# New prices in a list scheduler, and a third engine for the centring of rows: banded attention and a SoLU layer on one core

## The chip, the core and the metric

The kernel runs on one core of one Trainium2 chip. The core has a matrix engine (PE, with its weight loads listed apart as PEld), a vector engine (VectorE, DVE), an activation engine (ScalarE, ACT), GpSimd (POOL) and a sync engine (SP) that here issues loads. All run their own instruction streams in order and wait for each other by semaphores. The metric is the device time of one execution in microseconds (us), the median of several runs.

## The reference

Four batches of 8 heads with 768 positions and 64 columns each. A row of queries sees a band of 31 keys and, beside them, one summary key for each of 24 blocks of 32 positions (the maximum of the block's keys, with the mean of its values). The attention's output, 3072 rows of 512, goes through a layer with a softmax-weighted activation, a layer norm and a second product.

```python
k_sum = k.reshape(B, H, nb, 32, D).max(axis=3)
v_sum = v.reshape(B, H, nb, 32, D).mean(axis=3)
scores_l = where(abs(i - j) < 16, scale * q @ k.T, -1e9)
scores_s = scale * q @ k_sum.T + log(32)
a = softmax(concat([scores_l, scores_s]))
x = (a @ concat([v, v_sum])) as (3072, 512)
h = x @ w_in                                  # (3072, 1024)
solu = h * softmax(h)
mu = mean(solu); var = mean((solu - mu) ** 2)
out = ((solu - mu) / sqrt(var + 1e-6) * g_ln) @ w_out
```

## The kernel before

The 3072 rows are 24 tiles of 128. The kernel does not issue instructions as it meets them. Each step is recorded by `op(engine, cost, fn, ...)` as an operation with a planned cost in us, the buffers that it reads and writes, and at times other engines that could do it (`alt`, each with its own cost and function). At the end `Plan.issue` (L131) walks a planned clock: it takes the operation that can start first, on ties the one whose result is due first, gives it an engine and calls its function. So the costs decide two things, the order of the instructions in each engine's stream and which engine gets an operation that has a choice. They change no instruction's own duration on the chip.

An engine is passed over for an operation when another of its engines would have it done earlier, start plus cost plus a surcharge `DEAR` (L82, L154 to L166). An operation with `port=True` is one that VectorE, by the planner's assumption, can't run while GpSimd runs. Its planned cost on VectorE has the rest of GpSimd's current operation added, up to `HELD` (L150). A planned transfer ends by `RATE`. Until a planned time of `FILL` = 80 us, idle time of the matrix engine is filled with products of zeros (`keep_up`, L209; they appear in the profile as line L802).

The stages that matter:

- The loads, on SP's queue: keys and queries of batch 0, eight pieces of `w_in`, rows of values, then `w_out`.
- The weights come as 64-bit numbers, 16 pieces of 128x512. `rounded` (L313) makes 32-bit numbers of each: two scalings (L322, L328, on ScalarE or VectorE), a shift (L333) and a bit-wise combination (L337) on VectorE, and an integer add on GpSimd (L341, the only engine it has). Each `w_in` piece is then split in a high part (a copy with three helper lines, L245 to L247, one for each engine) and a low part (a subtraction by `tt`, L252 on VectorE or L253 on GpSimd). `w_out` is split by L363 and L365.
- Attention, for half a group of 256 positions at a time: `kw` gathers the windows of keys (`COPY_K`) and the maxima (`COPY_KS`), PE makes scores `s` (L505), VectorE masks them and takes maxima (L525), ScalarE takes exponentials (L533), and `e` is scaled by its sums (`MUL_E`, by `tt`: L252 on VectorE, L253 on GpSimd). Then PE turns it (`t`, L561) and makes `x` (L599).
- For a tile, `first(t)` (L613): `h` on PE (L625, 24 products), maximum (L632, VectorE), exponentials (L634, ScalarE), the product with its sum (L638, VectorE), minus the mean (`nmu`, L641), and then the centring: `he` plus `nmu` in two halves of 512 columns, each on GpSimd (L645) or VectorE (L647). ScalarE's squares (L650) follow. GpSimd takes a power (L655).
- `turn(t)` (lt, L561; lh, ll by L675) and `second(t)` (o, L690, 24 products) come three tiles later; the result leaves by L695 or L697 and a transfer from ScalarE's queue (L699).
- `add_rows` (L425) sums rows of values of the next batch on GpSimd, in halving steps.

The prices of the operations with a choice, before:

```python
COPY_W = ((act, 0.52), (dve, 0.34))
COPY_K = ((act, 0.74), (dve, 0.47))
COPY_KS = ((pool, 0.6), (dve, 0.19))
COPY_P = ((act, 0.48), (dve, 0.6))
LO_W = ((dve, 0.6), (pool, 1.4))
MUL_E = ((pool, 1.8), (dve, 1.07))
```

Of the kernel before, what the change touches and what calls it, by code (L numbers as in the profile page):

```python
# [31 lines left out]
WIN = QT + 2 * HALO  # L32
# [37 lines left out]
class Plan:  # L70
# [5 lines left out]

    RATE = 360.0
    START = 0.7
    COLD, FILL = 6.9, 80.0
    IDLE = 0.22  # L80
    WAIT, FAR = 1.5, 200
    DEAR = {"dve": 0.7, "act": 0.3}  # L82
    HELD = 1.1
    SYNC = 0.13
# [46 lines left out]
    def issue(self):  # L131
        ready, free, then, dma = {}, {}, {}, 0.0
        for o in self.ops:
# [87 lines left out]
def attn_then_solu(ctx: ExitStack, tc: tile.TileContext, q, k, v, vb, w_in, w_out, g_ln, out):  # L221
# [91 lines left out]
    def rounded(key, st, part):  # L313
# [32 lines left out]
    def split_w_in(c, nh):  # L346
        if nh == 0:
# [25 lines left out]
    def load_keys(b, p, after=()):  # L373
        pp, i = divmod(p, 2)
        if i == 0:
            kraw[b, pp] = plan.buf(sb, [P, 2, SP], F32, "kraw", 3, f"kraw{b}_{pp}")
        x = kraw[b, pp]
        op(sp, 0.05, lambda: nc.sync.dma_start(out=x.ap[:, i], in_=k[b, p]), w=[(x, i)], nbytes=P * SP * 4,
           after=after)
# [11 lines left out]
    def load_v_rows(b, i):  # L391

        rows = v[b, HALO + 2 * P * i:HALO + 2 * P * (i + 1), :].rearrange("(c p) n -> p c n", p=P)
        vst[b, i] = x = plan.buf(sb, [P, 2, 512], F32, "lh" if i < 2 else "ll", 2, f"st_v{b}_{i}")
        op(sp, 0.05, lambda: nc.sync.dma_start(out=x.ap, in_=rows), w=[x], nbytes=P * 4096)

# [16 lines left out]
    def add_rows(b, hh, i):  # L413

        x = plan.buf(sb, [P, 1024], F32, "vrow", 2, f"st_v{b}_{hh}_{i}")
        n, w = NB * 4, BLOCK * D // 2
        op(sp, 0.05, lambda w=w: nc.sync.dma_start(out=x.ap[:n, :w], in_=vb[b, hh, :, i * w:(i + 1) * w]),
           w=[x], nbytes=P * 4096)
# [29 lines left out]
    def load_q(b, g, pairs=None, after=()):  # L448
# [4 lines left out]
        if pairs is None:  # L453
            op(sp, 0.05, lambda: nc.sync.dma_start(out=x.ap, in_=src), w=[x], nbytes=P * 4096,
               after=after)
        else:
            op(sp, 0.05, lambda: nc.sync.dma_start(out=x.ap[:, pairs], in_=src[:, pairs]),
               w=[(x, pairs)], nbytes=P * 1024)

    def load_v(b, g, after=()):  # L460
        vt[b, g] = x = plan.buf(sb, [P, G, DM], F32, "vt", 2, f"vt{b}_{g}")
        rows = v[b, g * G * QT:g * G * QT + WIN, :]
        src = bass.AP(rows.tensor, rows.offset, [[DM, WIN], [QT * DM, G], [1, DM]])
        op(sp, 0.05, lambda: nc.sync.dma_start(out=x.ap[:WIN], in_=src), w=[(x, 0)], nbytes=WIN * 8192,
           after=after)
# [147 lines left out]
    def first(t):  # L613
# [29 lines left out]
        for hf in range(2):  # L643
# [3 lines left out]
               r=[nmu], w=[(e, hf)], alt=[(dve, 0.4, lambda sl=sl: nc.vector.tensor_scalar(  # L647
                out=e.ap[:, sl], in0=e.ap[:, sl], scalar1=nmu.ap, scalar2=None, op0=ALU.add))])
        sq = plan.buf(sb, [P, DF], BF16, "sq", 1, f"sq{t}")
# [30 lines left out]
    def second(t):  # L680
# [3 lines left out]
        for cols in [slice(0, 256), slice(256, 512)] if t == NT - 1 else [slice(0, DM)]:  # L684
            k = (cols.stop - cols.start) / DM
            o = plan.buf(ps, [P, DM], F32, "x", 2, f"o{t}")
            for f in range(NFC):
                def mm(f=f, w=wo[f], o=o, cols=cols):
# [24 lines left out]
    for x in LOADS:  # L713
        first_loads[x].pop(0)()
    op(sp, 0.05, lambda: nc.sync.dma_start(out=g_sb, in_=g_ln), w=[g_b], nbytes=P * 64)
    for pp in range(NPP):
# [121 lines left out]
```

## Time and profile before

| what | value |
|---|---|
| median of 3 runs | 412.13 us (410.32 to 412.26) |
| the profiled execution | 411.95 us, of which its span in the trace is 410.2 us |
| granted PE clock, mean | 0.988 |
| instructions | 9471 |
| PE, PEld busy | 392.3 us (96%), 302.7 us (74%) |
| DVE, ACT, POOL busy | 285.7 us (70%), 234.8 us (57%), 119.7 us (29%) |
| HBM read, written | 36.97 MB, 6.29 MB |

Busy time of PE has the products of zeros of L802 in it. The trace names a group of instructions by its line, engine and operation, then what it writes and reads. The time of an instruction that waits inside its engine, for a port say, counts as its duration. Idle time is told apart by what ended it (`<-`).

### The profile page before, as it was taken

Reading aid. Unit: us, or ns where it says so; the run is one execution under the profiler, and the core shown is the slowest. Engines: PE = TensorE matmul, PEld = TensorE weight load, DVE = VectorE, ACT = ScalarE, POOL = GpSimd, SP = SyncE. Lnnn points to the kernel's source line nnn. Section 1 sums busy time; section 2 is a strip of 40 time slices with the busy share of each in tenths; the row PEclk is TensorE's granted clock in tenths of the full one; section 3 lists DMA queues with packets and bytes.
Section 4 is the critical chain, followed back from the end, with each engine's and each line's share of the span. In section 5 each row is a group of like instructions: output and inputs, shape, how many; then the busy total and the mean of one; then the engine's idle time right before and its main releaser. Section 6 shows DMA issues by size and latency. Waiting matters only on the chain.

```text
span 410.2 us, 9471 instructions
## 1 busy us (share of the span) xinstructions
PE 392.3 (96%) x3666; PEld 302.7 (74%) x3666; DVE 285.7 (70%) x849; ACT 234.8 (57%) x704; POOL 119.7 (29%) x170
## 2 busy tenths in 40 slices
PE   6999798798999999999999999999999999999996
PEld 2436576576777777887788888887888888887776
DVE  4999898997667796657876766665684876455520
ACT  4967987765567666464654654746755464123321
POOL 4576545877573001011611111101101100111000
PEclk9998999998999999999999999999999999999999
DMA  8999995226444805017416023044030000000011
GB/s 264 410 269 270 329 267 159 93 78 193 121 137 126 212 27 153 2 41 202 120 51 166 2 81 99 24 103 98 27 95 29 26 2 27 27 26 25 2 51 53
DMA packets 22929, 46.03 MB, mean 112 GB/s; under 512 B 1860, under 2 KB 8260, under 8 KB 22884
## 3 DMA queue, kind: packets, MB, share of 16 engines
q1 hardware_dynamic: 18096, 36.97, 31.8%
q10 hardware_dynamic: 4788, 8.46, 6.5%
q8 instruction: 29, 0.48, 0.5%
q14 instruction: 16, 0.13, 0.1%
HBM read 36.97 MB, written 6.29 MB: 105 GB/s over the span
## 4 chain that ended last, share of the span: by engine, by line
PE 69%; DVE 8%; DMA 2%; ACT 2%; issue 0%; ACTq 0%; DVEq 0%
PE o L690 31%; PE h L625 25%; PE x L599 4%; PE s L505 4%; PE lt L561 3%; DMA kraw<-in_k 2%; PE t L561 2%; DVE ksum L387 2%; DVE hm L632 1%; PE vs_ps L440 1%; DVE cv_out L333 1%; DVE ll L675 1%; ACT e L533 1%; DVE e L525 1%; DVE w L365 1%; DVE he L638 1%
## 5 line engine op out<-in xcount | busy, mean ns | idle before, releaser
L625 PE MATMUL h<-w,xh 128*128 128x512 f32 x384 | 126.9, 400 | 5.3 <-DVE he L638 5.2
L690 PE MATMUL o<-w,lh 128*128 128x512 f32 (+1 forms) x400 | 128.3, 393 | 0.0
L533 ACT ACTIVATE e<-e,nm 128x120 f32<-128x120 f32 x192 | 73.1, 384 | 30.7 <-DVE nm L525 30.7
L625 PEld LDWEIGHTS h<-w,xh 128*128 128x128 f32 x384 | 72.7, 189 | 24.2 <-DVE he L638 4.1
L690 PEld LDWEIGHTS o<-w,lh 128*128 128x128 f32 x400 | 74.0, 188 | 18.8 <-issue 2.4
L690 PE MATMUL o<-w,ll 128*128 128x512 f32 (+1 forms) x200 | 77.4, 387 | 0.0
L625 PE MATMUL h<-w,xl 128*128 128x512 f32 x192 | 76.0, 396 | 0.0
L645 POOL TENSOR_SCALAR he<-he,nmu 128x512 f32<-128x512 f32 x23 | 20.9, 909 | 119.0 <-DVE nmu L641 109.4
L245 ACT COPY at<-t 120x512 f32<-120x512 f32 x47 | 25.2, 587 | 47.4 <-PE t L561 46.3
L632 DVE TENSOR_REDUCE hm<-h 128x1 f32<-128x1024 f32 x24 | 29.3, 1221 | 25.9 <-PE h L625 25.9
L690 PEld LDWEIGHTS o<-w,ll 128*128 128x128 f32 x200 | 37.6, 188 | 7.4
L650 ACT ACTIVATE sq<-he 128x1024 bf16<-128x1024 f32 x24 | 25.4, 1058 | 29.8 <-POOL he L645 16.7
L625 PEld LDWEIGHTS h<-w,xl 128*128 128x128 f32 x192 | 36.4, 189 | 7.9
L525 DVE CUSTOM_DVE_ANT_0 e<-s,mask 128x120 f32<-128x120 f32 x192 | 40.6, 275 | 2.3 <-PE s L505 2.3
L675 DVE TENSOR_TENSOR ll<-lt,lh 128x512 fp32r<-128x512 f32 x48 | 31.9, 684 | 8.1 <-ACT lh L245 7.6
L533 ACT ACTIVATION_READ_ACCUMULATOR e<-e,nm 128x1 f32 x192 | 36.4, 190 | 0.0
L425 POOL TENSOR_TENSOR st_v<-st_v 96x512 f32<-96x512 f32 (+3 forms) x42 | 32.1, 778 | 12.6 <-DMA st_v<-in_vb 12.0
L634 ACT ACTIVATE he<-h,hm 128x1024 f32<-128x1024 f32 x24 | 27.0, 1126 | 10.8 <-DVE hm L632 10.7
L638 DVE SCALAR_TENSOR_TENSOR he<-h,hz,he 128x1024 f32<-128x1024 f32 x24 | 30.6, 1277 | 0.2
L599 PE MATMUL x<-at,vt 120*64 120x64 f32 (+1 forms) x768 | 29.5, 230 | 0.7 <-ACT at L245 0.6
L599 PEld LDWEIGHTS x<-at,vt 120*64 120x64 f32 (+1 forms) x768 | 25.5, 141 | 6.1 <-issue 2.6
L247 POOL COPY kw<-ksum 128x192 f32<-128x192 f32 (+1 forms) x26 | 8.7, 337 | 71.9 <-ACT lh L245 31.7
(80 smaller groups left out, 513.2 us busy)
## 6 DMA issues: line engine op xcount, KB each, us to landing
vt<-in_v SPq DMA_DIRECT2D x12, 768.0 KB, 5.9
kraw<-in_k SPq DMA_DIRECT2D x16, 400.0 KB, 4.6
out<-os ACTq DMA_DIRECT2D x23, 256.0 KB, 2.0
qt<-in_q SPq DMA_DIRECT2D x11, 512.0 KB, 7.2
st_v<-in_vb SPq DMA_DIRECT2D x12, 384.0 KB, 4.9
raw<-in_w_in SPq DMA_DIRECT2D x8, 512.0 KB, 7.5
raw<-in_w_out SPq DMA_DIRECT2D x8, 512.0 KB, 12.7
vt<-vsum ACTq DMA_DIRECT2D x11, 192.0 KB
```

What stands on the lines that cost most here:

```text
L245: by = {act: lambda: nc.scalar.copy(out=to(), in_=of()), dve: lambda: nc.vector.tensor_copy(out=to(), in_=of()), pool: lambda: nc.gpsimd.t ...
L425: op(pool, 0.15 + w * 0.0021, lambda w=w, o=o: nc.gpsimd.tensor_tensor(out=o.ap[:n, :w], in0=x.ap[:n, :w], in1=x.ap[:n, w:2 * w], op=ALU.add),
L525: nc.vector.tensor_tensor_reduce(out=e.ap[:, n, :], in0=sc.ap[:, j, (2 * i + up) * KC:(2 * i + up + 1) * KC], in1=mask[:, mi, :], scale=-S ...
L533: nc.scalar.activation(out=e.ap[:, n, :], in_=e.ap[:, n, :], func=AF.Exp, bias=nm.ap[:, n:n + 1], scale=-1.0, accum_out=z.ap[:, n:n + 1])
L599: nc.tensor.matmul(xp.ap[j * D:(j + 1) * D, i, qs], vs.ap[:k, u, cs], at.ap[:k, u % 2, n[j] + u // 2, :], start=not apart, stop=not apart ...
L625: nc.tensor.matmul(o, a.ap[:, c, ts], w.ap[:, i], start=(c == 0 and n == 0), stop=(c == NKC - 1 and n == 2))
L632: op(dve, 1.13, lambda: nc.vector.tensor_reduce(out=nm.ap, in_=h.ap, op=ALU.max, axis=AX.X, negate=True), r=[h], w=[nm])
L634: op(act, 1.09, lambda: nc.scalar.activation(out=e.ap, in_=h.ap, func=AF.Exp, bias=nm.ap, accum_out=z.ap), r=[h, nm], w=[e, z])
L638: op(dve, 1.27, lambda: nc.vector.scalar_tensor_tensor(out=e.ap, in0=h.ap, scalar=z.ap, in1=e.ap, op0=ALU.mult, op1=ALU.mult, accum_out=s1 ...
L650: op(act, 1.13, lambda: nc.scalar.activation(out=sq.ap, in_=e.ap, func=AF.Square, accum_out=ss.ap), r=[e], w=[sq, ss])
L675: op(dve, 0.6, lambda part=part, r=r: nc.vector.tensor_tensor(out=part(lo), in0=tp.ap[:, r], in1=part(hi).bitcast(F32), op=ALU.subtract), ...
L690: nc.tensor.matmul(o.ap[:, cols], a.ap[:, f, :], w.ap[:, i, cols], start=(f == 0 and n == 0), stop=(f == NFC - 1 and n == 2))
```

## The change

It has three parts.

1. The transfers. The planned rate goes from one value to two (270 up to a planned 6.9 us, 400 after it), a transfer's tail from 0.8 to 0.6, and the cost of issuing one from 0.05 to 0.43 us on SP's queue and from 0.06 to 0.34 or 0.8 on ScalarE's.
2. The port. VectorE's port operations are charged the whole rest of GpSimd's operation, and GpSimd's operations the rest of VectorE's last port operation (`held`). More of VectorE's operations count as port operations: L337, the low parts of both weights, the centring. `DEAR` goes from 0.7 to 0.6 for VectorE, stays 0.3 for ScalarE and is 1.0 for GpSimd, which had none.
3. The centring has a third choice, an `activation` with a bias on ScalarE, at 0.57.

```diff
-    RATE = 360.0
+    RATE, SLOW = 400.0, 270.0
-    DEAR = {"dve": 0.7, "act": 0.3}
-    HELD = 1.1
+    DEAR = {"dve": 0.6, "act": 0.3, "pool": 1.0}
...
         def cost(e, o, t):
-            held = min(max(free.get("pool", 0.0) - t, 0.0), self.HELD) if e == "dve" and o.port else 0.0
-            return o.can[e][0] * (2 if e == "pe" and t < self.COLD else 1) + held
+            other = free.get("pool", 0.0) if e == "dve" and o.port else held if e == "pool" else 0.0
+            return o.can[e][0] * (2 if e == "pe" and t < self.COLD else 1) + max(other - t, 0.0)
...
             o.end = free[e] = t + cost(e, o, t)
+            if e == "dve" and o.port:
+                held = o.end
             if o.nbytes:
-                dma = max(dma, o.end + 1.0) + o.nbytes / self.RATE * 1e-3
-                o.end = dma + 0.8
+                dma = max(dma, o.end + 1.0)
+                dma += o.nbytes / (self.RATE if dma > self.COLD else self.SLOW) * 1e-3
+                o.end = dma + 0.6
...
-        op(sp, 0.05, lambda: nc.sync.dma_start(out=x.ap, in_=src.bitcast(I32)), w=[x], nbytes=P * 4096,
+        op(sp, 0.43, lambda: nc.sync.dma_start(out=x.ap, in_=src.bitcast(I32)), w=[x], nbytes=P * 4096,
...
         op(dve, 0.6, lambda: nc.vector.scalar_tensor_tensor(
             out=low(), in0=high(), scalar=-2 ** 31, in1=low(), op0=ALU.bitwise_and, op1=ALU.bitwise_or),
-            r=[(x, 1)], w=[(x, 0)])
+            r=[(x, 1)], w=[(x, 0)], port=True)
...
         tt(LO_W, ALU.subtract, lambda: hl.ap[:, 1], w, lambda: hl.ap[:, 0].bitcast(F32),
-           r=[(st, nh), (hl, 0)], w=[(hl, 1)])
+           r=[(st, nh), (hl, 0)], w=[(hl, 1)], port=True)
...
-            op0=ALU.mult, op1=ALU.subtract), r=[(st, f % 2), (hl, 0), g_b], w=[(hl, 1)])
+            op0=ALU.mult, op1=ALU.subtract), r=[(st, f % 2), (hl, 0), g_b], w=[(hl, 1)], port=True)
...
-        return op(act, 0.06, lambda: nc.scalar.dma_start(
+        return op(act, 0.8, lambda: nc.scalar.dma_start(
...
                r=[nmu], w=[(e, hf)], alt=[(dve, 0.4, lambda sl=sl: nc.vector.tensor_scalar(
-                out=e.ap[:, sl], in0=e.ap[:, sl], scalar1=nmu.ap, scalar2=None, op0=ALU.add))])
+                out=e.ap[:, sl], in0=e.ap[:, sl], scalar1=nmu.ap, scalar2=None, op0=ALU.add)),
+                (act, 0.57, lambda sl=sl: nc.scalar.activation(
+                    out=e.ap[:, sl], in_=e.ap[:, sl], func=AF.Identity, bias=nmu.ap))], port=True)
...
-            op(act, 0.06, lambda os=os, cols=cols: nc.scalar.dma_start(
+            op(act, 0.34, lambda os=os, cols=cols: nc.scalar.dma_start(
```

The other loads on SP's queue change from 0.05 to 0.43 in the same way.

More of the change, by code (lines that the diff above doesn't have):

```diff
@@ L131, in issue @@
     def issue(self):
-        ready, free, then, dma = {}, {}, {}, 0.0
+        ready, free, then, dma, held = {}, {}, {}, 0.0, 0.0
         for o in self.ops:
@@ L377, in load_keys @@
         x = kraw[b, pp]
-        op(sp, 0.05, lambda: nc.sync.dma_start(out=x.ap[:, i], in_=k[b, p]), w=[(x, i)], nbytes=P * SP * 4,
+        op(sp, 0.43, lambda: nc.sync.dma_start(out=x.ap[:, i], in_=k[b, p]), w=[(x, i)], nbytes=P * SP * 4,
            after=after)
@@ L394, in load_v_rows @@
         vst[b, i] = x = plan.buf(sb, [P, 2, 512], F32, "lh" if i < 2 else "ll", 2, f"st_v{b}_{i}")
-        op(sp, 0.05, lambda: nc.sync.dma_start(out=x.ap, in_=rows), w=[x], nbytes=P * 4096)
+        op(sp, 0.43, lambda: nc.sync.dma_start(out=x.ap, in_=rows), w=[x], nbytes=P * 4096)
     def mean_values_first(b):
@@ L416, in add_rows @@
         n, w = NB * 4, BLOCK * D // 2
-        op(sp, 0.05, lambda w=w: nc.sync.dma_start(out=x.ap[:n, :w], in_=vb[b, hh, :, i * w:(i + 1) * w]),
+        op(sp, 0.43, lambda w=w: nc.sync.dma_start(out=x.ap[:n, :w], in_=vb[b, hh, :, i * w:(i + 1) * w]),
            w=[x], nbytes=P * 4096)
@@ L453, in load_q @@
         if pairs is None:
-            op(sp, 0.05, lambda: nc.sync.dma_start(out=x.ap, in_=src), w=[x], nbytes=P * 4096,
+            op(sp, 0.43, lambda: nc.sync.dma_start(out=x.ap, in_=src), w=[x], nbytes=P * 4096,
                after=after)
         else:
-            op(sp, 0.05, lambda: nc.sync.dma_start(out=x.ap[:, pairs], in_=src[:, pairs]),
+            op(sp, 0.43, lambda: nc.sync.dma_start(out=x.ap[:, pairs], in_=src[:, pairs]),
                w=[(x, pairs)], nbytes=P * 1024)
@@ L463, in load_v @@
         src = bass.AP(rows.tensor, rows.offset, [[DM, WIN], [QT * DM, G], [1, DM]])
-        op(sp, 0.05, lambda: nc.sync.dma_start(out=x.ap[:WIN], in_=src), w=[(x, 0)], nbytes=WIN * 8192,
+        op(sp, 0.43, lambda: nc.sync.dma_start(out=x.ap[:WIN], in_=src), w=[(x, 0)], nbytes=WIN * 8192,
            after=after)
@@ L714, in attn_then_solu @@
         first_loads[x].pop(0)()
-    op(sp, 0.05, lambda: nc.sync.dma_start(out=g_sb, in_=g_ln), w=[g_b], nbytes=P * 64)
+    op(sp, 0.43, lambda: nc.sync.dma_start(out=g_sb, in_=g_ln), w=[g_b], nbytes=P * 64)
     for pp in range(NPP):
```

## The prediction

> **What bounds the kernel now.** I read the page's first part for the shares, then the windows, to see whether one limit holds all along.
>
> ```profile
> span 410.2 us, 9471 instructions
> ...
> 10.00:94.00 84.00, 73.85 (x691) 48.33 (x684) 80.21 (x195) 65.49 (x186) 53.67 (x53) 0.96 0.79 232
> ...
> 94.00:100.00 6.00, 6.00 (x87) 4.82 (x86) 4.00 (x21) 2.58 (x5) 3.33 (x6) 0.72 0.64 169
> 100.00:400.00 300.00, 298.83 (x2789) 240.29 (x2788) 197.65 (x625) 161.14 (x506) 57.76 (x91) 1.00 0.27 74
> 400.00:410.20 10.20, 7.08 (x55) 6.55 (x53) 0.00 (x0) 1.64 (x3) 0.00 (x0) 1.00 0.15 53
> ```
>
> After the width the columns are busy PE, PEld, DVE, ACT, POOL, then granted clock, share of the DMA engines and GB/s. There are two regimes. From 100 to 400 PE is idle for 1.17 of 300 us, so no order of the other engines can save more than that there. From 10 to 94 VectorE is busy for 80.21 of 84 us, and PE's 73.85 has products of zeros in it. The chain of waits and PE's waits say the same:
>
> ```profile
> 71.73 2.89 DVE cv_out L333
> ...
> 92.26 1.30 DVE he L638 x2
> 93.56 0.14 issue
> 93.70 1.24 PE h L625 x3
> ```
>
> ```profile
> PE h L625 <- DVE he L638: 5.2, 3, 1.9
> ```
>
> Up to 93.70 the chain that ends last runs on VectorE, then on PE, and the first tiles' `h` wait for the product L638 that frees the one `h` buffer. Since PE's work behind that point is fixed, the end moves about as far as VectorE's stage ends earlier or later. The change has to be judged there.
>
> VectorE's time in this stage is not all work. VectorE's rows, then GpSimd's (start, duration; in brackets the idle time before it and what ended it):
>
> ```profile
> 12.71 0.68 DVE L337 SCALAR_TENSOR_TENSOR raw<-raw 128x512 int32<-128x512 int32 x1
> 15.41 2.28 DVE L337 SCALAR_TENSOR_TENSOR raw<-raw 128x512 int32<-128x512 int32 x1
> 20.88 2.00 DVE L252 TENSOR_TENSOR e<-e,z 128x960 f32<-128x960 f32 x1
> 23.40 0.42 DVE L333 TENSOR_SCALAR cv_in<-raw 128x512 int32<-128x512 int32 x1
> 25.77 1.78 DVE L337 SCALAR_TENSOR_TENSOR raw<-raw 128x512 int32<-128x512 int32 x1
> 27.47 1.51 DVE L333 TENSOR_SCALAR cv_in<-raw 128x512 int32<-128x512 int32 x1
> 28.91 1.78 DVE L337 SCALAR_TENSOR_TENSOR raw<-raw 128x512 int32<-128x512 int32 x1
> 35.77 0.68 DVE L252 TENSOR_TENSOR w<-cv_in,w 128x512 fp32r<-128x512 f32 x1
> 40.90 1.25 DVE L333 TENSOR_SCALAR cv_out<-raw 128x512 int32<-128x512 int32 x1
> 71.65 2.97 DVE L333 TENSOR_SCALAR cv_out<-raw 128x512 int32<-128x512 int32 x1
> 86.26 1.21 DVE L647 TENSOR_SCALAR he<-he,nmu 128x512 f32<-128x512 f32 x1
> ```
>
> ```profile
> 15.29 1.86 POOL L253 TENSOR_TENSOR e<-e,z 128x960 f32<-128x960 f32 x1 [0.17 <-DVE z L539]
> 20.54 1.32 POOL L253 TENSOR_TENSOR w<-cv_in,w 128x512 fp32r<-128x512 f32 x1 [1.37 <-ACT raw L322]
> 25.59 1.41 POOL L341 TENSOR_TENSOR cv_in<-cv_in,raw 128x512 int32<-128x512 int32 x1 [0.63 <-DVE raw L337]
> 26.96 3.18 POOL L253 TENSOR_TENSOR w<-cv_in,w 128x512 fp32r<-128x512 f32 x2
> 40.57 1.30 POOL L253 TENSOR_TENSOR w<-cv_in,w 128x512 fp32r<-128x512 f32 x1 [1.76 <-ACT w L245]
> 71.22 1.78 POOL L253 TENSOR_TENSOR e<-e,z 128x960 f32<-128x960 f32 x1
> 72.98 1.35 POOL L645 TENSOR_SCALAR he<-he,nmu 128x512 f32<-128x512 f32 x2
> 85.39 1.79 POOL L253 TENSOR_TENSOR e<-e,z 128x960 f32<-128x960 f32 x1
> ```
>
> L337 takes 0.68 with GpSimd idle and 1.78 when it starts 0.18 behind an add of 1.41: it sits out GpSimd's instruction. At 71.65 a shift of 0.42 lasts 2.97, through one product and two centrings on GpSimd.
>
> **The change part by part.** *Which work changes engine.* The rule adds the surcharge to the cost. Low parts: GpSimd 1.4 + 1.0 against VectorE 0.6 + 0.6 (before 1.4 against 1.3). Scaling of `e`: 1.8 + 1.0 against 1.07 + 0.6 (before 1.8 against 1.77). Maxima into `kw`: 1.6 against 0.79 (before 0.6 against 0.89). Centring: GpSimd 1.62, VectorE 1.0, ScalarE 0.87 (before 0.62 and 1.1). GpSimd now needs VectorE busy with non-port work for 1.2, 1.1 or 0.8 us to win one of these. I take it that all of them leave GpSimd in this stage and that a tile's first half is centred on ScalarE and its second on VectorE. What stood there:
>
> ```profile
> L253 POOL TENSOR_TENSOR e<-e,z 128x960 f32<-128x960 f32 x4 | 7.2, 1804 | 1.6 <-DVE z L539 1.6
> L253 POOL TENSOR_TENSOR w<-cv_in,w 128x512 fp32r<-128x512 f32 x4 | 5.8, 1460 | 3.1 <-ACT w L245 1.8 <-ACT raw L322 1.4
> ...
> L645 POOL TENSOR_SCALAR he<-he,nmu 128x512 f32<-128x512 f32 x3 | 2.0, 689 | 0.0
> L247 POOL COPY kw<-ksum 128x192 f32<-128x192 f32 x5 | 1.7, 345 | 4.7 <-DVE ss L652 2.4 <-PE s L505 2.2
> ```
>
> ```profile
> 133.98 1.16 DVE L252 TENSOR_TENSOR e<-e,z 128x960 f32<-128x960 f32 x1
> ```
>
> *Stage A, 14 to 42 us, the `w_in` weights.* GpSimd's adds and VectorE's L333 and L337 exclude each other, so the two engines' port times add up. Four low parts go from 1.46 to 0.68 (the row at 35.77) and one `e` from 1.80 to 1.16 (the row at 133.98): 4 x 0.78 + 0.64 = 3.8 off. Counted on VectorE alone, it sheds the waits at 15.41, 20.88, 27.47, 28.91 and 40.90, 1.60 + 0.84 + 1.09 + 1.10 + 0.83 = 5.5, and takes 4 x 0.68 + 1.16 = 3.9, so only 1.6 is off. I take 3.8: the rows from 25.59 to 28.91 show one engine waiting out the other, back to back.
>
> *Stage B, 42 to 94.* Here VectorE is the chain. It sheds 2.97 - 0.42 = 2.55 at 71.65 and 1.21 - 0.42 = 0.8 at 86.26. It takes three `e` of 1.16 and five `kw` copies for which VectorE has no row (at least L333's 0.42 scaled from 512 to 192 columns, 0.16, at most GpSimd's 0.345; I take 0.2, nearer to the row of the same engine): 3.5 + 1.0. One centring half of five goes, 0.4. Sum: 0.7 added. Counted by the port, three `e` at 0.64, three centrings at 0.69 and 0.7 of copies would be 4.7 off. I take 0.7 added, as the chain here names VectorE alone.
>
> *The third engine.* A half on ScalarE is a 128x512 activation; the nearest row says 0.68:
>
> ```profile
> L322 ACT ACTIVATE raw<-raw 128x512 f32<-128x512 f32 x12 | 8.2, 682 | 1.2 <-DMA raw<-in_w_in 0.6 <-DMA raw<-in_w_out 0.6
> ```
>
> Some 24 halves are 16 us more for ScalarE, most of them after 100 us, where it is busy for 161 of 300. It waits for `nmu`, and behind it in ScalarE's queue stand exponentials, copies of `at` and `xh`, on which PE waits. PE's cover is that these are ordered ahead of need; with the cover gone one such wait costs up to its 0.7. I count none, bound 3 for four of them.
>
> *Issue and transfers.* No transfer is added and SP's queue has the same instructions; its real issue time was there already. Only the plan's clock is nearer to it, so VectorE may be given other work in place of waiting:
>
> ```profile
> DVE raw L324 <- DMA raw<-in_w_out: 1.6, 2, 1.2
> ```
>
> The gain is between 0 and 1.6; I take half, 0.8. ScalarE's issues are dearer in the plan, which with VectorE's cheaper 0.6 tips some copies of keys (1.04 against 1.07, before 1.17) and of `at` to VectorE. In stage A and B that may add up to five copies of 0.6, 3 us; GpSimd's rest, now charged in full, pulls the other way, and I take 0.
>
> *The clock.* PE's fill ends at a planned 80 us, and the plan's clock runs nearer to the chip's now.
>
> ```profile
> 92.00:94.00 2.00, 0.30 (x1) 0.30 (x2) 1.90 (x6) 0.87 (x2) 2.00 (x7) 1.00 0.30 102
> 94.00:96.00 2.00, 2.00 (x24) 1.32 (x24) 1.86 (x7) 1.15 (x2) 0.84 (x2) 0.54 0.86 248
> ```
>
> After the 1.9 us wait before 93.70 the clock is 0.54, and 0.72 over the six us from 94: 6 x 0.28 = 1.7 lost. This may go, stay or come twice; I take that it stays, bounds 1.7 either way. The Trainium skill, "TensorE: Matmul & The Clock Gate", Part 1, says the clock falls only after an idle window of about 3.4 us. By that rule a gap of 1.9 us alone costs nothing and the bounds shrink to zero; the row at 94 speaks against reading it so, and the row decides.
>
> *Sum.* -3.8 + 0.7 - 0.8 = -3.9 on the span: 406.3. The profiled execution was 411.95 at its span of 410.2, so 1.75 lies around it: 408.05. That execution stands 0.18 below the median of 412.13, so I say 408.1. What tells a change of this kernel from none is about 0.5%, 2.1 us.
>
> **The rivals.** *The port stays full (no change).* GpSimd-only adds (L341) and row sums slide into the places that were freed and VectorE waits for those instead; stage A then gives the 1.6 counted on VectorE alone, stage B +0.7, and the waits for weights stay. 410.2 - 0.9 + 1.75 = 411.1. For it: the row at 25.77 shows VectorE waiting out an add that can't move. Against: GpSimd has 53.67 busy us in 84, and 16.7 of them leave.
>
> *The plan fits better (much faster).* Both stages by the port, 3.8 + 4.7, with all of the 1.6 waits and the clock's 1.7: 11.8 off, 400.2. For it: an order that knows the stretched durations starts the right step. Against: the rule takes what can start first, so it moves an operation to another engine but never holds it back until the port is free.
>
> *VectorE is overloaded (slower).* VectorE takes 3.9 + 3.5 + 1.0 and, if half of the 5.5 + 3.35 that it sheds comes back behind other GpSimd work, saves only 4.4; with 0.4 for a half centred elsewhere the stage grows by 3.6, to 415.6, and with the copies up to 418.6. It decides as soon as less than 8.0 of waiting goes. For it: VectorE is already at 80.21 of 84. Against: in stage A the waits that end are longer than the work that comes.
>
> *The change does not act.* If planned backlogs still favour GpSimd, or ScalarE is never the cheapest, the instructions stay where they are: 412. The price gaps of 0.8 to 1.2 us speak against it; it is counted with no change.
>
> **How the numbers follow.** The forecast's case, 404 to 410: 0.44. Much faster, under 404: 0.16. No change, 410.1 to 414.2: 0.22. Slower, above 414.2: 0.18. Faster by over 0.5% is 0.44 + 0.16 = 0.60. The predicted time is 408.1; the range from 401.5 to 415 leaves about 0.05 below and 0.15 above. The likeliest case alone reaches from 404 to 410.
>
> **What would show it.** The first tile's `h` starts here:
>
> ```profile
> 38.30 0.79 PE L625 MATMUL h<-w,xh 128*128 128x512 f32 x1
> ```
>
> Right: no or few L253 and L645 rows on GpSimd before 94 us; an activation for `he` with about 24 entries at 0.68; L337's and L333's means nearer to 0.68 and 0.42; `h` of the first tile earlier than 38.30 and PE without gaps from about 90 us, not 94. Wrong: L337 as long as now behind L341; VectorE's share up to 94 us unchanged with a later end; more PE waits for ScalarE after 100 us, above the 1.17 us; a second stretch at half clock.

## The result and the profile after

The changed kernel takes 423.39 us (median of 4 runs, 421.13 to 425.39); beside it the kernel before took 411.85 us (4 runs, 410.32 to 412.26). The ratio is 1.0286, 95% interval 1.022 to 1.0351: slower by about 11.8 us by that ratio (11.5 between the medians), outside the predicted range of 401.5 to 415. The profiled execution was 422.2 us at a span of 419.9.

The first part of the page, then the windows (columns as in the prediction):

```profile
span 419.9 us, 9538 instructions
...
PE 396.9 (95%) x3706; PEld 306.5 (73%) x3706; DVE 286.0 (68%) x870; ACT 244.2 (58%) x717; POOL 90.1 (21%) x136
```

```profile
10.00:94.00 84.00, 73.08 (x694) 48.21 (x693) 63.78 (x178) 66.40 (x187) 32.33 (x25) 0.96 0.72 224
94.00:100.00 6.00, 5.18 (x39) 3.83 (x37) 4.16 (x7) 1.11 (x2) 4.79 (x6) 1.00 0.29 93
100.00:400.00 300.00, 294.05 (x2817) 236.98 (x2818) 209.36 (x665) 169.57 (x519) 48.49 (x85) 1.00 0.28 77
400.00:419.90 19.90, 16.78 (x109) 14.34 (x107) 4.21 (x9) 3.05 (x6) 0.00 (x0) 1.00 0.14 54
```

Up to 94 us VectorE's busy time fell from 80.21 to 63.78 us and GpSimd's from 53.67 to 32.33. So the port was relieved, by more than was forecast, and the kernel is slower all the same. VectorE now stands idle for 84 - 63.78 = 20.2 us where it stood for 3.8. From 100 to 400 us PE is idle for 5.95 us, against 1.17.

The groups of VectorE between 10 and 94 us, then GpSimd's and ScalarE's rows of the whole span (count, busy, mean ns, idle before and releaser):

```profile
L339 DVE SCALAR_TENSOR_TENSOR raw<-raw 128x512 int32<-128x512 int32 x16 | 14.1, 888 | 0.0
L335 DVE TENSOR_SCALAR cv_out<-raw 128x512 int32<-128x512 int32 x8 | 5.6, 711 | 0.0
L254 DVE TENSOR_TENSOR w<-cv_in,w 128x512 fp32r<-128x512 f32 x8 | 5.5, 690 | 14.0 <-ACT w L247 14.0
L254 DVE TENSOR_TENSOR e<-e,z 128x960 f32<-128x960 f32 x4 | 4.6, 1149 | 0.0
```

```profile
L249 POOL COPY kw<-ksum 128x192 f32<-128x192 f32 x21 | 7.9, 376 | 78.9 <-PE s L507 44.0 <-ACT lh L247 20.4 <-ACT xh L247 14.5
...
L255 POOL TENSOR_TENSOR e<-e,z 128x960 f32<-128x960 f32 x2 | 3.8, 1881 | 0.0
```

```profile
L651 ACT ACTIVATE he<-he,nmu x14: 708/724/736, 68.8 to 396.8; 128x512 f32<-128x512 f32 x14
```

All eight low parts are on VectorE, at 690 ns, and GpSimd keeps 2 scalings of `e`. The copies of maxima stay on GpSimd, and ScalarE centres 14 halves, where 24 were expected. The low parts brought 14.0 us of waiting for ScalarE with them.

Where the time goes shows in the start of a tile's maximum `hm`, which follows its last product of `h`. First and second tile, before:

```profile
45.87 1.21 DVE L632 TENSOR_REDUCE hm<-h 128x1 f32<-128x1024 f32 x1
60.37 1.22 DVE L632 TENSOR_REDUCE hm<-h 128x1 f32<-128x1024 f32 x1
```

and after:

```profile
54.23 1.22 DVE L634 TENSOR_REDUCE hm<-h 128x1 f32<-128x1024 f32 x1
73.40 1.22 DVE L634 TENSOR_REDUCE hm<-h 128x1 f32<-128x1024 f32 x1
```

The first tile is 8.4 us late, the second 13.0. By the same rows the fifth is 7.4 late, the eighth 10.9 and the end of the span 9.7. Three losses, then: one inside the first tile's `h`, one between the first and second tile, and one between the fifth tile and the eighth, whose maxima start at 111.72 and 161.84. Between the second and the fifth some 5.6 us are won back. From the eighth tile on the two kernels run in step.

**The first tile.** Windows of 10 us, before and then after:

```profile
20.00:30.00 10.00, 9.10 (x47) 3.07 (x45) 9.97 (x12) 6.76 (x12) 7.13 (x5) 1.00 1.08 277
30.00:40.00 10.00, 10.00 (x126) 6.69 (x126) 10.00 (x17) 6.92 (x12) 6.68 (x6) 0.83 1.05 265
40.00:50.00 10.00, 7.66 (x79) 5.91 (x79) 8.40 (x38) 9.01 (x32) 4.74 (x4) 0.99 0.99 326
```

```profile
20.00:30.00 10.00, 8.53 (x42) 2.54 (x41) 4.90 (x10) 5.44 (x10) 5.43 (x3) 1.00 1.07 288
30.00:40.00 10.00, 9.88 (x126) 6.63 (x126) 5.58 (x9) 6.83 (x12) 1.11 (x1) 0.83 0.97 236
40.00:50.00 10.00, 6.93 (x42) 4.86 (x41) 5.29 (x16) 7.47 (x14) 3.31 (x4) 1.00 0.83 311
50.00:60.00 10.00, 6.87 (x110) 5.15 (x109) 8.32 (x34) 10.00 (x41) 5.05 (x4) 1.00 1.02 309
```

VectorE, nearly full before, works about half of the 30 us from 20 to 50 now. The DMA engines are busy for 0.83 to 1.07 and move 236 to 311 GB/s, where the plan now counts on 400. The rows of the trace after that show what VectorE and PE wait for (ScalarE, then VectorE, GpSimd and PE; idle time before in brackets):

```profile
30.07 0.58 ACT L413 COPY vsum<-vs_ps 24x512 f32<-24x512 f32 x1 [2.55 <-PE vs_ps L409]
30.67 0.62 ACT L247 CAST w<-cv_in 128x512 fp32r<-128x512 f32 x1
...
36.56 0.59 ACT L247 CAST xh<-x 128x512 fp32r<-128x512 f32 x1 [0.29 <-PE x L601]
...
43.54 0.68 ACT L324 ACTIVATE raw<-raw 128x512 f32<-128x512 f32 x1 [2.35 <-DMA raw<-in_w_out]
...
50.43 0.60 ACT L247 CAST w<-cv_in 128x512 fp32r<-128x512 f32 x1
```

```profile
31.32 0.69 DVE L254 TENSOR_TENSOR w<-cv_in,w 128x512 fp32r<-128x512 f32 x1 [6.42 <-ACT w L247]
```

```profile
38.89 1.42 POOL L343 TENSOR_TENSOR cv_in<-cv_in,raw 128x512 int32<-128x512 int32 x1 [10.35 <-DVE raw L339]
```

```profile
38.26 0.79 PE L627 MATMUL h<-w,xh 128*128 128x512 f32 x1
...
46.89 0.50 PE L627 MATMUL h<-w,xh 128*128 128x512 f32 x1 [2.53 <-DVE w L254]
```

I read it as a chain of streams that can't overtake; which of its links count is tried below. ScalarE's copy of the value sums waits for PE and loads until 30.07; the cast of a weight's high part stands behind it; VectorE's low part waits 6.42 us for that cast; the shifts and combinations of the last three weights stand behind the low part, so GpSimd's add is idle for 10.35 us before 38.89. Then the last casts of `w_in` stand on ScalarE behind scalings of `w_out`, which wait for their load (2.35 us at 43.54). `h` starts on time, at 38.26 (before: 38.30), and its last products wait for the last low parts.

### The profile page after: what moved, and what is told of

The parts are those of the page before. It is cut to its first block, busy times and chain, and to the rows that moved or that the text cites. A ratio compares the mean times of both kernels' runs of the same rounds, so it can differ in the third digit from the quotient of the medians.

```text
span 419.9 us, 9538 instructions
## 1 busy us (share of the span) xinstructions
PE 396.9 (95%) x3706; PEld 306.5 (73%) x3706; DVE 286.0 (68%) x870; ACT 244.2 (58%) x717; POOL 90.1 (21%) x136
## 4 chain that ended last, share of the span: by engine, by line
PE 60%; ACT 1%; DVE 1%; issue 0%
PE o L694 27%; PE h L627 21%; PE x L601 4%; PE s L507 3%; PE lt L563 2%; PE t L563 2%; PE vs_ps L442 0%; ACT e L535 0%; ACT he L636 0%; DVE e L254 0%; DVE hm L634 0%; ACT os L699 0%; ACT at L247 0%; ACT z L540 0%; DVE z L541 0%
## 5 line engine op out<-in xcount | busy, mean ns | idle before, releaser
L659 POOL TENSOR_TENSOR y<-ss,mhalf 128x1 f32<-128x1 f32 x24 | 13.4, 560 | 172.1 <-DVE ss L656 170.5
L247 ACT COPY at<-t 120x512 f32<-120x512 f32 x38 | 20.8, 588 | 45.2 <-PE t L563 43.8
L427 POOL TENSOR_TENSOR st_v<-st_v 96x512 f32<-96x512 f32 (+3 forms) x42 | 33.3, 804 | 14.8 <-DMA st_v<-in_vb 10.2
L601 PE MATMUL x<-at,vt 120*64 120x64 f32 (+1 forms) x768 | 30.4, 230 | 4.6 <-ACT at L247 3.0
L507 PE MATMUL s<-kw,qt 64*64 64x120 f32 x768 | 26.5, 275 | 3.6 <-DVE nm L527 1.4
```

The costliest lines, as they stand in the source:

```text
L427: op(pool, 0.15 + w * 0.0021, lambda w=w, o=o: nc.gpsimd.tensor_tensor(out=o.ap[:n, :w], in0=x.ap[:n, :w], in1=x.ap[:n, w:2 * w], op=ALU.add),
L507: nc.tensor.matmul(sc.ap[cu * QT:(cu + 1) * QT, j, n * KC:(n + 1) * KC], qs.ap[j * D:(j + 1) * D, 2 * pp + i, u * QT:(u + 1) * QT], kw.ap[ ...
L601: nc.tensor.matmul(xp.ap[j * D:(j + 1) * D, i, qs], vs.ap[:k, u, cs], at.ap[:k, u % 2, n[j] + u // 2, :], start=not apart, stop=not apart ...
```

## The experiments

The tables of the runs name the ratio to the kernel before, run on the same chip, with its 95% interval. "Late" is the start of a tile's `hm` in the profiled run against the profiled run of before.

**One part of the change undone.** Four kernels, each the changed one with one part put back (the main lines of each diff; `...` stands for the rest).

```diff
 no_port: the port's charging and its marks as before
-            other = free.get("pool", 0.0) if e == "dve" and o.port else held if e == "pool" else 0.0
+            held = min(max(free.get("pool", 0.0) - t, 0.0), self.HELD) if e == "dve" and o.port else 0.0
...
 no_dear:
-    DEAR = {"dve": 0.6, "act": 0.3, "pool": 1.0}
+    DEAR = {"dve": 0.7, "act": 0.3}
 no_transfer: the rate, the tail and all issue costs as before
-    RATE, SLOW = 400.0, 270.0
+    RATE = 360.0
...
 no_centre: ScalarE's choice taken away
-                (act, 0.57, lambda sl=sl: nc.scalar.activation(
```

> The changed kernel with the port's charging as it was (capped at 1.1, GpSimd not charged, the new port flags gone); new surcharges, transfer costs and ScalarE's centring stay. Theory A (the full charging of the port orders the w_in stage badly: VectorE's low parts that wait for ScalarE stand ahead of conversions that are ready): most of the loss goes, 408 to 414 us, and the first tile's maximum (hm) starts at 45 to 48 us in place of 54.2. Theory B (the transfers' new costs) and theory C (GpSimd's surcharge, which moves the low parts to VectorE): 420 to 425, first maximum at 53 to 55. Theory D (ScalarE's centring): 420 to 425.

> The changed kernel with the surcharges as they were (VectorE 0.7, ScalarE 0.3, GpSimd none); the rest of the change stays. Theory A (port charging): still slow, 419 to 426, first maximum at 53 us or later. Theory C (the surcharge that moves low parts to VectorE): 408 to 414 with some low parts back on GpSimd and the first maximum at 45 to 48. Theories B and D: 420 to 425.

> The changed kernel with the costs of issue, rate and tail of transfers as they were; the rest stays. Theory B (the plan takes loads for too early, so PE's sums of value rows and ScalarE's copy of them stand in front of ready work): 408 to 414, first maximum at 45 to 48. Theories A, C and D: 418 to 425, first maximum at 52 to 55.

> The changed kernel without ScalarE as a choice for the centring; the rest stays. Theory D (centrings in ScalarE's queue hold up copies that PE waits for): 410 to 415. Theories A, B and C: 420 to 425 with the first maximum at 54 us as in the changed kernel, since nothing in the w_in stage is touched.

| run | median us | ratio | interval | 1st, 2nd tile late | span late |
|---|---|---|---|---|---|
| no_port | 424.65 | 1.0335 | 1.0268 to 1.0402 | 2.7, 7.4 | 12.8 |
| no_dear | 426.25 | 1.0375 | 1.0293 to 1.0457 | 14.0, 14.1 | 14.3 |
| no_transfer | 418.56 | 1.0189 | 1.0112 to 1.0266 | 5.3, 9.0 | 6.0 |
| no_centre | 427.04 | 1.0388 | 1.0318 to 1.0457 | 9.4, 12.2 | 16.2 |

Only taking the transfers' costs back seems to help, by about a third of the loss (1.89% for 2.86%; the two intervals overlap). The other three leave the loss or add to it. The 408 to 415 us that I expected of the part at fault came for none of them, and `no_dear` and `no_centre` lie above all their ranges. The parts don't add up, and each of the four has an order of its own. `no_port` shows how little one stage says: its first tile is only 2.7 us late and its end 12.8.

**One part alone, on the kernel before.**

```diff
 centre_alone:
+                (act, 0.57, lambda sl=sl: nc.scalar.activation(
+                    out=e.ap[:, sl], in_=e.ap[:, sl], func=AF.Identity, bias=nmu.ap))
 transfer_alone:
-    RATE = 360.0
+    RATE, SLOW = 400.0, 270.0
...
-        op(sp, 0.05, ...)
+        op(sp, 0.43, ...)
...
```

> The kernel before with ScalarE as a third choice for the centring and nothing else. Theory A2: no harm, first maximum at 46 us as before, 408 to 414. Theory D (centrings in ScalarE's stream delay what PE waits for): 414 to 420 with new gaps between 100 and 170 us.

> The kernel before with only the transfers' new costs (issue, rate, tail). Theory A3 (early loads harm only when the adds are planned late as well, which the port charging and the surcharge do): 408 to 413, first maximum at 45 to 48. Theory B alone (the transfers' costs harm by themselves): 415 to 422.

The centring alone: 409.71 us, 0.9973 (0.9942 to 1.0005), no change that can be told. The transfers' new costs alone: 421.98 us, 1.0259 (1.0198 to 1.032), first and second tile 1.1 and 8.6 late, span 9.2. The time lies in the range of theory B (415 to 422). Only planned numbers differ from the kernel before, so this part alone makes a loss of nearly the whole size, through the order and the choice of engines that the planner draws from them. It does not all come early: the fifth tile of `transfer_alone` is only 2.5 us late, the eighth 9.9.

**Single late steps moved.** The changed kernel with a few steps set elsewhere in one engine's stream, all other streams kept: `low_later` puts five of VectorE's steps behind its last combination of `w_in`, `copy_later` puts ScalarE's copy of the value sums and its transfer behind the last scaling of `w_in`, `casts_first` puts three of ScalarE's casts ahead of the scalings of `w_out`; `both_later` and `all_moved` combine two and three of these.

```diff
+        order = self.moved(order)
...
 low_later:
+    MOVES = (((("low", 4), ("low", 6), ("xl", 0, 0, 0), ("low", 1), ("xl", 0, 0, 1)), ("mix", 7)),)
 copy_later:
+    MOVES = ((("vsum", "v2"), ("s2", 7)),)
 casts_first:
+    MOVES = (((("hi", 3), ("hi", 5), ("hi", 7)), ("kw", 0, 2, 0)),)
```

> The changed kernel with five steps of VectorE (the low parts of w_in pieces 4, 6 and 1 and the two subtractions of the first x) put behind the bit-wise combination of the last piece in VectorE's stream; all else in its planned place and engine. Theory A2 (VectorE's in-order stream lost its time at 25 to 38 us because these steps wait for ScalarE in front of conversions that are ready): GpSimd's idle time of 10.35 us before the sixth add goes, the first tile's maximum starts at 47 to 50 in place of 54.2, and the time is 414 to 418. Rival (the loss comes from the plan after 100 us, not from the weights): first maximum earlier, time 419 to 424.

> The changed kernel with ScalarE's copy of the value sums (and the transfer behind it) put behind the scaling of the last w_in piece, so that casts and scalings no longer stand behind PE's late sums; VectorE's order stays. Theory A2: no gain by itself, 419 to 424 and a first maximum at 53 to 55, since VectorE still waits for the subtractions of x. Rival (ScalarE's wait for the sums alone is the cause): 412 to 416, first maximum at 47 to 49.

> Both moves together. Theory A2: the w_in stage is cured, first maximum at 45 to 47.5 and PE's gaps before 60 us back to about 27 to 29 us in place of 34; the time is 411 to 415, what is left being the gaps between 100 and 170 us. Rival (the loss comes later): 418 to 423.

> The changed kernel with ScalarE's last three casts of w_in (pieces 3, 5, 7) put ahead of its scalings of w_out in ScalarE's stream, nothing else moved. Theory A3 (with both earlier moves the eighth add ended at 34 us and the casts still ran at 45.7 to 51.2, because they stand behind w_out scalings that wait for their loads): the casts follow their adds, the last low part ends at 45 to 46.5 us in place of 51.8, the first maximum is at 47.5 to 49.5 and the time is 415 to 420. Rival (VectorE's stream alone sets the weights' end): no earlier first maximum, 53 to 55.

> The three moves together (five VectorE steps later, the copy of the value sums later, the three casts ahead of the w_out scalings). Theory A3: all eight adds end by 35 us, the casts follow, the first maximum is at 42 to 46 and the time is 409 to 414, with what is left in the gaps after 100 us. Rival (the loss is decided after 100 us whatever the weights do): first maximum as early, time 418 to 423.

| run | median us | ratio | interval | 1st, 2nd tile late | span late |
|---|---|---|---|---|---|
| low_later | 423.68 | 1.0316 | 1.0264 to 1.0368 | 9.1, 13.8 | 9.9 |
| copy_later | 421.83 | 1.0282 | 1.0245 to 1.0319 | 9.6, 12.3 | 9.5 |
| both_later | 423.94 | 1.0316 | 1.0255 to 1.0377 | 8.5, 14.1 | 11.9 |
| casts_first | 423.21 | 1.0304 | 1.0236 to 1.0371 | 3.6, 12.5 | 10.8 |
| all_moved | 421.46 | 1.0241 | 1.0177 to 1.0306 | 1.9, 12.1 | 10.1 |

These were my first account of the loss, and they refute it as the whole. Of the chain in the first tile only the last link shows by itself: the casts set ahead take that tile from 8.4 us late to 3.6, while the low parts and the copy moved, alone or together, leave it at 8.5 to 9.6, though `low_later` and `both_later` were expected to cure it. With all three moves it is 1.9 late. But the second tile stays 12.1 late and the end 10.1: what the first tile won is lost again before the second. PE in `all_moved`:

```profile
53.95 1.88 PE L537 MATMUL s<-kw,qt 64*64 64x120 f32 x32 [6.55 <-DMA qt<-in_q]
```

These are the third group's first scores, and they wait for their q load. In TensorE's order they stand ahead of the second tile's `h`; before, they stood behind it. The second tile's `h` has to wait with them. The changed kernel has the same order, but with its first tile 8.4 us late these scores wait for VectorE and not for the load:

```profile
54.58 1.05 PE L507 MATMUL s<-kw,qt 64*64 64x120 f32 x32 [1.12 <-DVE nm L527]
```

**The planned rate.** `rate_300` is the changed kernel, `tr_rate300` is `transfer_alone`, each with one number changed. `cen_rate300` is `centre_alone` with 300 in place of its 360.

```diff
-    RATE, SLOW = 400.0, 270.0
+    RATE, SLOW = 300.0, 270.0
```

> The changed kernel with the planned rate at 300 in place of 400 once past the first 6.9 us; nothing else. Theory A3 with theory B (the plan takes the w_out loads for 5 to 10 us too early and so puts their scalings in front of the casts): the casts stand ahead by the plan itself, first maximum at 46 to 50, 413 to 419. Theory C or the port charging alone: 420 to 425, first maximum at 53 or later.

> The kernel before with the transfers' new costs alone (issue 0.43, ScalarE's issues 0.8 and 0.34, landing 0.6 behind, 270 up to 6.9 us), but a planned rate of 300 in place of 400 from there on; TensorE's order has the third group's scores behind the second tile's h, as before. Theory A (of the transfers' costs the rate alone does the harm, because the queue moves about 240 to 330 GB/s where loads stand in line): 408 to 413 us, 9 to 14 us under the run with 400. Rival B (the issue costs on SyncE's and ScalarE's queues do it): 418 to 423 us, as with 400.

> The kernel before with ScalarE's choice for the centrings and a planned rate of 300 in place of 360; no other cost is changed. Theory A (a later planned landing keeps work that is ready ahead of work that waits): as the centrings alone or a little faster, 406 to 411 us. Rival B (a plan that thinks the loads late puts other work off, and TensorE starts tiles later): 411 to 416 us, since the first maxima would start up to 5 us later.

| run | median us | ratio | interval | 1st, 2nd tile late | span late |
|---|---|---|---|---|---|
| rate_300 | 415.57 | 1.0102 | 1.0034 to 1.017 | 3.2, 5.0 | 2.8 |
| tr_rate300 | 411.26 | 1.0024 | 0.9984 to 1.0065 | 1.4, 1.2 | -1.5 |
| cen_rate300 | 417.15 | 1.0144 | 1.0056 to 1.0232 | 1.1, 0.9 | 3.8 |

`rate_300` and `tr_rate300` lie in the ranges of the theories that blame the rate (413 to 419 and 408 to 413). Among the transfers' new costs the rate does the harm: with the same issue costs and 300 the loss of 2.6% is gone. In the changed kernel the lower rate takes back 7.6 of the 11.8 us (1.84 of 2.86%). The rate of 400 was not run with the old issue costs. In the plan the third group's q load lands at 44.06 us by the rate of 400 and at 55.52 by 300. On the chip it is issued here in `transfer_alone` (one of two), and PE's scores wait for it until 54.42:

```profile
45.21 0.93 SPq L455 DMA_DIRECT2D qt<-in_q  x2
```

```profile
54.42 1.88 PE L506 MATMUL s<-kw,qt 64*64 64x120 f32 x32 [4.01 <-DMA qt<-in_q]
```

The rate of 400 has the load land before the chip has issued it. The 360 of the kernel before is hardly better: its plan has that load land at 46.08, and its trace has it issued at 45.75 at the earliest. That the kernel before had the good order was luck, within 2 us of planned time, as `q_ahead` below shows. In `tr_rate300` the last product of the second tile's `h` and then the scores, with no wait:

```profile
59.50 0.39 PE L626 MATMUL h<-w,xh 128*128 128x512 f32 x1
59.96 0.69 PE L562 MATMUL t<-ident,e 64*120 64x64 f32 x16
60.58 1.05 PE L506 MATMUL s<-kw,qt 64*64 64x120 f32 x32
```

A later rate is no cure by itself. `cen_rate300` has the scores in the right place as well and keeps the first ten tiles within 2 us, but loses 2.29 us of PE and a stretch of lower clock (0.82 over 7 us) near 203 us, where PE's scores wait for VectorE's copy of `at`:

```profile
202.78 1.05 PE L505 MATMUL s<-kw,qt 64*64 64x120 f32 x32 [2.29 <-DVE at L246]
```

```profile
205.00:212.00 7.00, 7.00 (x27) 5.58 (x26) 6.11 (x26) 4.28 (x19) 1.42 (x2) 0.82 0.42 147
```

It came out slower, as its rival said, but above the rival's 411 to 416 us, and the place that the rival named (the first maxima) was not the one.

**One load's planned landing.** `q_ahead` is the kernel before, with the third group's q load planned to land 2 us earlier (at 44.08; the change has 44.06). `q_behind` is the changed kernel, with that load planned 10 us later. No other number differs, but the planner makes all that follows this place anew.

```diff
             op(sp, 0.05, lambda: nc.sync.dma_start(out=x.ap, in_=src), ...)
+            plan.ops[-1].late = -2.0 if (b, g) == (0, 2) else 0.0     # q_behind: 10.0
...
+                o.end += getattr(o, "late", 0.0)
```

> The kernel before with one number changed: the planned landing of the third group's q load (qt0_2) is 2.0 us earlier, 44.08 where it was 46.08, as early as the changed kernel has it; every cost and every other load is priced as before. In TensorE's order the third group's first scores then stand ahead of all eight steps of the second tile's h, where they stood behind them. Theory A (a planned landing that is too early puts work that waits for a load ahead of work that is ready, and this one place carries most of the loss): the second tile's h starts 6 to 10 us later than before, a gap by the q load of 3 to 7 us on TensorE at 50 to 60, time 417 to 423 us. Rival B (the loss comes from many small displacements and not from this place): the q load's wait is taken up elsewhere, 410 to 414 us. Rival C (the place matters, but what it loses is won back, since h of the second tile would wait anyway): 412 to 415 us.

> The changed kernel with one number changed: the planned landing of qt0_2 is 10 us later (54.06 for 44.06); all else as in the change. The third group's first scores go behind the second tile's h. Theory A: the wait for the q load ahead of that h goes; the second tile's maxima are then late only by what the first tile's are (about 8 us, from the casts of w_in and the copy of the value sums), and the end comes 3 to 8 us earlier than in the changed kernel: 415 to 420 us. Rival B: what the first tile lost at 20 to 50 us is the whole loss, and the scores' place only hides in it: 422 to 425 us.

`q_ahead`: 415.25 us, 1.0091 (1.0048 to 1.0134), first and second tile 2.3 and 7.4 late, span 4.0. `q_behind`: 420.07 us, 1.0218 (1.0134 to 1.0303), 6.6 and 10.1 late, span 8.0 (changed kernel: 9.7). PE in `q_ahead`:

```profile
57.65 1.88 PE L507 MATMUL s<-kw,qt 64*64 64x120 f32 x32 [3.19 <-DMA qt<-in_q]
```

So the place is a cause: put into the good order, it costs 3.7 us (0.91%), with all that the plan makes of it later; the range that I gave for its carrying most of the loss (417 to 423) was missed. Part of the delay is won back: the second tile is 7.4 late, the end 4.0. Taken out of the bad order, its 3.3 us (423.39 to 420.07) lie inside the intervals of the two ratios, and the second tile stays 10.1 late where about 8 was expected, so this side agrees without deciding. By `q_ahead` the place is worth about a third of the loss. Other waits lie between 100 and 160 us, where PE stands idle for 4.5 us in the changed kernel and for 0.4 before. The longest is at 105, ahead of the fifth tile's maximum. GpSimd's row sums wait for a late load of values, with PE behind them:

```profile
100.60 3.25 POOL L427 TENSOR_TENSOR st_v<-st_v 96x512 f32<-96x512 f32 x5 [1.44 <-DMA st_v<-in_vb]
```

```profile
105.27 0.63 PE L442 MATMUL vs_ps<-vacc,ident 96*24 96x64 f32 x8 [2.44 <-POOL vacc L431]
```

In `transfer_alone` ScalarE's squares wait for a centring on GpSimd, the copies of `at` stand behind them, PE runs dry and its clock falls:

```profile
131.66 1.06 ACT L651 ACTIVATE sq<-he 128x1024 bf16<-128x1024 f32 x1 [2.83 <-POOL he L646]
```

```profile
133.33 0.48 PE L600 MATMUL x<-at,vt 120*64 120x64 f32 x4 [2.79 <-ACT at L246]
```

```profile
134.00:141.00 7.00, 6.95 (x70) 5.47 (x71) 4.38 (x37) 5.14 (x25) 0.35 (x1) 0.58 0.74 192
```

That is 2.8 us of waiting and 7 x 0.42 = 2.9 of clock, together more than half of the 9.2 us that this kernel's span is late. Which planned time puts these later steps there was not tried.

**The port and the centring at a rate of 300.** `port_rate300` adds the port's charging and its marks to `tr_rate300`, without the new surcharges; `cen_tr_rate300` adds the centring on ScalarE. The diffs are those of the change.

> tr_rate300 (transfers' new costs, planned rate 300) plus the change's charging of the shared port: VectorE charged for all of GpSimd's time and GpSimd for VectorE's, three steps and the centring marked as using the port; surcharges as before, no centring on ScalarE. This is the forecast's main term with the transfers' rate taken out of it. Theory A (the forecast's port term holds once the plan's loads land when the chip's do): the low parts and half-tile scalings off GpSimd save 1 to 4 us of VectorE's waits, 406 to 410 us. Rival B (VectorE is handed more work than it gains, the last low part of w_in and with it the last step of the first tile's h come later, 46.3 for 43 in the plan): 412 to 416 us, with the first maxima 2 to 4 us later than in tr_rate300. Rival C (nothing either way): 410 to 412 us.

> tr_rate300 with ScalarE's choice for the centrings added; port and surcharges as before. Theory A (the centrings alone were worth about -2 us and the rate 300 with the new issue costs about 0, and the two add): 407 to 411 us, the lowest of these kernels. Rival B (a small change of costs puts some other step behind a wait, as cen_rate300 did from 190 us on): 412 to 418 us.

`port_rate300`: 412.67 us, 1.0055 (1.0021 to 1.009). `cen_tr_rate300`: 411.18 us, 1.0024 (0.999 to 1.0058). Neither beats the kernel before; the centring makes no difference again, and the sum that I expected for it did not come. The windows of `tr_rate300` and `port_rate300`:

```profile
10.00:94.00 84.00, 75.57 (x706) 49.01 (x708) 82.43 (x190) 64.34 (x184) 54.36 (x49) 0.98 0.73 230
```

```profile
10.00:94.00 84.00, 79.67 (x733) 52.12 (x732) 72.74 (x177) 64.43 (x185) 45.28 (x40) 0.96 0.76 229
```

The port's charging takes 9.7 us off VectorE and 9.1 off GpSimd, with the third group's scores behind the second tile's `h` again, and the kernel is not faster. What VectorE waits for then, in `port_rate300` (ScalarE, VectorE):

```profile
33.05 0.58 ACT L413 COPY vsum<-vs_ps 24x512 f32<-24x512 f32 x1 [4.05 <-PE vs_ps L409]
...
37.56 0.58 ACT L247 CAST xh<-x 128x512 fp32r<-128x512 f32 x1 [1.31 <-PE x L601]
```

```profile
38.18 0.69 DVE L607 TENSOR_TENSOR xl<-x,xh 128x512 fp32r<-128x512 f32 x1 [4.29 <-ACT xh L247]
```

The first tile's `x` comes from the value sums: loads of values, PE's sums and ScalarE's copy. Part of VectorE's relief is spent waiting for it, 4.29 us in this row. What follows is rival B of this run, with its range (412 to 416), its later maxima (2.6 and 2.4 us behind `tr_rate300`) and its mechanism: seven of the eight low parts are on VectorE now, and the last one, with the last products of `h` and the maximum behind it, comes late (in `tr_rate300` it ends at 41.85 on GpSimd, and the maximum starts at 47.28):

```profile
46.54 1.65 DVE L254 TENSOR_TENSOR w<-cv_in,w 128x512 fp32r<-128x512 f32 x1
48.24 0.50 PE L627 MATMUL h<-w,xh 128*128 128x512 f32 x1
49.84 1.17 DVE L634 TENSOR_REDUCE hm<-h 128x1 f32<-128x1024 f32 x1
```

## Why the prediction was wrong, by its steps

*What bounds the kernel.* The fixed work of PE behind 100 us held for the most part (5.95 us idle there). That the end moves with VectorE's stage did not hold. The chain of waits that I quoted reaches back to 71 us; I carried VectorE's part in it over to the stretch from 14 us by its busy share. There its waits for the port cost the first tile nothing, since another chain came last. The first product of `h` started at 38.30 before, at 38.26 after with 10.0 us less of VectorE's busy time from 10 to 40 us (29.9 and 20.0), and `xh` was cast at 36.60 and 36.56. The rows that showed it were in the trace of before (ScalarE, PE):

```profile
36.60 0.58 ACT L245 CAST xh<-x 128x512 fp32r<-128x512 f32 x1 [0.76 <-PE x L599]
```

```profile
44.31 0.40 PE L625 MATMUL h<-w,xh 128*128 128x512 f32 x1
```

`h` starts when `x` is there and runs through to this last product without a wait, with the last low part done at 41.87 (the prediction's row at 40.57). Weights that were ready sooner had nothing to give to the first tile; weights that came later could only cost.

*Which work changes engine.* Right for the low parts and nearly so for `e`; wrong for the maxima's copies, and 14 halves in place of 24 for the centring. The combination's mean fell from 1138 to 888 ns, not to 0.68 us; the integer adds stay on GpSimd. So the signs that I named for the change of engines came in part, while those that were tied to the time did not: `h` starts no earlier, and PE waits more after 100 us, which I had named as a sign of being wrong.

*Stages A and B, -3.8 and +0.7.* The relief came (VectorE 16.4 us less up to 94 us), but not its worth: by `port_rate300` against `tr_rate300` the port's charging makes about +1 us, two intervals that overlap, in place of -3.1. Time off VectorE's stream was counted as time off the end, though the last low part came later by it. "The port stays full" came nearest to the size of this term, for a wrong reason: the port was relieved.

*Issue and transfers, -0.8.* The step that failed. I wrote that the plan's clock comes nearer to the chip's, and bounded the term by the waits that could go, 0 to 1.6 us of gain. The issue costs do come nearer (the first q loads' issues take 0.42 and 0.43 us in the trace of before, and `tr_rate300` is harmless), but the rate goes away from the chip: 400 against 236 to 326 GB/s between 20 and 60 us in the rows of both kernels. I had quoted 232 GB/s for 10 to 94 us and did not hold it against the rate. A bound for a loss through the order was missing altogether (the 3 us that I allowed were for copies that ScalarE's dearer issues move to VectorE): a step that waits for a load, ordered ahead of ready work on an engine that can't overtake, can cost up to the lateness of the load. By the runs the whole term is about +10.7 by itself (2.59% of the 411 to 412 us of before), and the rate is worth 7.6 of the 11.8 in the change.

*The clock, 0.* The stretch of lower clock at 94 us went (0.72 to 1.00), which the bounds allowed for. The Trainium skill, "TensorE: Matmul & The Clock Gate", Part 1, has the clock fall after an idle window of about 3.4 us. Here a shorter wait was enough: 2.79 us in `transfer_alone`, then 0.58 over 7 us. A wait of 2.44 at 105 us in the changed kernel left the clock at 1.00.

*The centring on ScalarE, none counted.* Right twice, in `centre_alone` and `cen_tr_rate300`; in `no_centre` the interval overlaps with that of the change.

*The rivals.* The slower one, VectorE overloaded, had a side of the result but neither its size (415.6 to 418.6) nor its mechanism: VectorE's busy time up to 94 us fell. Its mechanism is nearer to what `port_rate300` showed. No rival was about the order that a too early landing makes, though the change altered that number.

*What stays open.* That the rate makes 7.6 of the 11.8 us is shown by changing it, and one of its places by `q_ahead`. How the rest of that loss arises at the other places is read from traces and not tried. Why the port, the surcharges and the centring together cost 6 to 8 us with the old transfers (`no_transfer`) and about 4 with the rate of 300 (`rate_300`) is not taken apart; the surcharges were not run alone.

## What to carry to other kernels

In a planner, a price does two things, and here the order was the dearer one: an engine that runs its stream in order can pay a load's lateness for work that was ready behind it, so hold a planned rate, and the planned landings that follow from it, against the trace before anything else. A rate that is nearer to the trace is no cure by itself, as `cen_rate300` shows. An engine at 95% busy need not be the bound while its durations hold waits: look for what starts the next stage (here `x`) and what ends it (here the last low part), and ask which of them the change moves. Undoing parts of a reordering change one by one did not split its loss; changing one planned number priced one place, though the plan behind it changed with it.

## What was not expected of the hardware

The rate of the loads falls while the DMA engines stay about as busy: 410 GB/s from 10 to 20 us in the traces of before and after, 236 to 326 from 20 to 60, at a busy share of 1.02 and 0.83 to 1.08. The loads of the two stretches are not the same ones, and what makes the difference was not tried. And PE's clock can pay as much for a wait as the wait itself: in `transfer_alone` 2.79 us of waiting, then 2.9 us lost at 0.58.
